# One transfer for the second group's x, and four tap products ahead of an eviction, in a fused convolution and channel-MLP kernel

## The chip, the cores and the metric

The kernel runs on one core of a Trainium2 chip. A core has five engines that run their own instruction streams: TensorE (PE, matrix products into PSUM), VectorE (DVE), ScalarE (ACT), GpSimd (POOL) and SyncE (SP, which here only issues transfers). Transfers between the chip's memory (HBM) and the core's SBUF run on 16 DMA engines; SP's transfers and POOL's transfers stand in different queues. The metric is the time of one execution on the device in microseconds (us), as a median over runs. In the profile "PEld" is TensorE's loading of weights.

## The reference

`x` is 8 x 4224 x 192 in 32-bit floats. First a causal depthwise convolution with 7 taps, whose weights are a softmax over the taps of each of 8 heads (a head is 24 neighbouring channels); then a channel MLP on the normalized result, added to it:

```
w = exp(weight - max(weight)); w = w / (sum(w) + 1e-9)          # 8 heads x 7 taps
conv[b, s, h, :] = sum over k of w[h, k] * x[b, s + k - 6, h, :]  # zero where s + k < 6
mu, var = mean and variance of conv over its 192 channels
xn  = (conv - mu) / sqrt(var + 1e-6) * g_ln
out = conv + max(xn @ w_ch1, 0) @ w_ch2                          # 192 -> 768 -> 192
```

## The kernel before

**Groups.** The sequence is cut into 18 groups of up to 16 positions on each of 128 partitions. For the whole batches a partition holds 32 neighbouring positions, which makes 4096 of the 4224; the remaining 128 positions of all eight batches together are the second group (group 1): 8 batches x 16 partitions x 8 positions. Its x is therefore not one plain run of rows: batch b goes to partitions 16b to 16b + 15, and each partition's row has its 8 positions and the 6 before them, 14 x 192 numbers or 10,752 bytes. The first group (group 0) has 6 positions, group 2 has 10, all later ones 16.

**The stages of a group.** x is loaded (`load_x`, line 133). The convolution is built up in a tile `y`: ACT writes the first tap's product for each head (`first_tap`, line 369, its instruction on line 378), and DVE adds the further taps, one instruction for each tap and head (`conv`, line 409, its instruction on line 415). DVE transposes `y` into `yt` (line 426). `up` (line 559) multiplies with the first weights in six slices f = 0 to 5 (line 531). Each slice fills four of the eight PSUM banks; ACT applies the ReLU and moves it to SBUF (`evict_up`, line 507, its instruction on line 521); slice f + 2 uses the banks of slice f. `down` (line 800, its product on line 798) multiplies with the second weights `w2`. From group 3 on other routines take this place (`up_mixed`, `down_fast`, line 861).

**The order.** The schedule is written out by hand: each engine runs its instructions in the order in which the code issues them, and waits on semaphores for what it needs. SP and POOL issue their transfers in order too; a transfer whose conditions are not met holds up those behind it.

**The start.** The weights arrive as 64-bit floats and are rebuilt as 32-bit ones on DVE and ACT (`split_words`, `scale_power`, `join_low`, `join_sign`, `join_product`, lines 231 to 268). For `w2` this happens beside the first group's `up`: its words are loaded at line 990, on SP just ahead of x for group 1 (line 994), into `raw2`. `scale_power` for `w2` is one ACT instruction (line 246), which `join_sign` on DVE needs, and which in turn comes before the product that writes `w2` (line 264).

**What ACT does beside `up(0)`.** Between the evictions of the first group's six slices ACT also evicts four copies of `w1` (`copies_of_w1`, line 348, whose products stand between slices f1 and f2 on PE and use the banks of f0 and then free them for f3), runs `scale_power` for `w2`, and makes the first tap's products of group 1, for two heads behind f0, for two behind f1, for four behind f3.

**What DVE does beside it.** `join_low`, then the taps 1 to 4 of group 1 for heads 0 and 1, then the same for heads 2 and 3 (the loop on line 1031), `join_sign` and `join_product` for `w2`, taps 5 and 6 of heads 0 to 3, the transposition of the first half of group 1's `y`, all taps of heads 4 to 7, and the second half's transposition.

**x for group 1.** `load_x(1, gate=True)` first writes one element of each partition on DVE (line 139), which the transfers then wait for, so that they start only behind DVE's earlier work. Then it issues eight transfers of 16 partitions each (line 142), those of batches 0 to 3 on SP and those of batches 4 to 7 on POOL. SP's next transfers are the store of group 0's `y` (line 487) and x for group 2 (line 151).

Of the kernel before, what the change touches and what calls it, by code (L numbers as in the profile page):

```python
# [16 lines left out]
def kernel(  # L17
# [29 lines left out]
    nc = tc.nc  # L47
    PSUM = bass.MemoryType.PSUM
    B, S, D = x.shape
    H, K = weight.shape  # L50
    F = moe_w_ch1.shape[1]
    P = 128
# [3 lines left out]
    PAD = K - 1  # L56
    J = 16
    R = 2 * J
    LEFT = (S - P * R) * B // P
    LP = P // B  # L60
# [64 lines left out]
    def take_set():  # L125
        i = (turn[0] + 3) // 4 * 4 % 8
        turn[0] = i + 4
        return all_banks[:, i : i + 4]
# [4 lines left out]
    def load_x(g, queue=nc.sync, pad=True, gate=False):  # L133
        b, j0, n = groups[g]
        t = xpool.tile([P, J + PAD, D], F32, tag="xg", name=f"xg{g}")
        xg[g] = t
        flat = t.rearrange("p j d -> p (j d)")
        if gate:
            nc.vector.memset(t[0 : 1 if b is not None else P, 0:1, 0:1], 0.0)
        if b is None:  # L140
            for b in range(B):
                (queue if b < B // 2 else nc.gpsimd).dma_start(
                    out=flat[LP * b : LP * b + LP, 0 : (PAD + n) * D],
                    in_=bass.AP(
                        tensor=x.tensor, offset=(b * S + P * R - PAD) * D,
                        ap=[[n * D, LP], [1, (PAD + n) * D]],
                    ),
                )
            return
        if j0:  # L150
            queue.dma_start(
                out=flat[:, 0 : (n + PAD) * D], in_=xr[b, :, (j0 - PAD) * D : (j0 + n) * D]
            )
            return
        if b:

            queue.dma_start(
                out=flat[:, 0 : (PAD + n) * D],
                in_=bass.AP(
                    tensor=x.tensor, offset=(b * S - PAD) * D, ap=[[R * D, P], [1, (PAD + n) * D]]  # L160
                ),
            )
            if pad:
                nc.gpsimd.memset(t[0:1, 0:PAD, :], 0.0)
            return
        nc.gpsimd.memset(t[0:1, 0:PAD, :], 0.0)
        for p0, p1 in ((16, P), (1, 16)):
            nc.sync.dma_start(  # L168
                out=flat[p0:p1, 0 : (PAD + n) * D],
                in_=bass.AP(  # L170
                    tensor=x.tensor, offset=(b * S + p0 * R - PAD) * D,
                    ap=[[R * D, p1 - p0], [1, (PAD + n) * D]],
                ),
            )
        nc.sync.dma_start(out=flat[0:1, PAD * D : (PAD + n) * D], in_=xr[b, 0:1, 0 : n * D])
# [38 lines left out]
    for s in range(2):  # L214
        nc.sync.dma_start(  # L215
            out=raw1[:, s].rearrange("p f w -> p (f w)"),
            in_=w1_words[0:P, 2 * FH * s : 2 * FH * (s + 1)],
        )
    for r in range(2):
        nc.sync.dma_start(  # L220
            out=raw1[Q * r : Q * r + Q, 2, :, :].rearrange("p f w -> p (f w)"),
            in_=w1_words[P:D, 2 * FH * r : 2 * FH * (r + 1)],
        )
    load_x(0)


# [18 lines left out]
    def scale_power(power):  # L245
        nc.scalar.activation(power, power, AF.Relu, scale=float(1 << 23), bias=low)
# [52 lines left out]
    for q in range(NQ):  # L299
        m = copy[C * q : C * q + C].rearrange("p (q i) -> p q i", q=NQ)  # L300
        nc.gpsimd.affine_select(
            out=m, in_=m, pattern=[[0, NQ], [-1, C]],
# [9 lines left out]
        out=unit, in_=unit, pattern=[[-1, P]], compare_op=ALU.not_equal, fill=1.0, base=0,  # L312
# [56 lines left out]
    def first_tap(g, heads=(0, H)):  # L369
        n = groups[g][2]  # L370
        if g == 1:

            y[g] = y[0][:, groups[0][2] :]
        elif heads[0] == 0:
            y[g] = ypool.tile([P, J, D], F32, tag="y", name=f"y{g}")
        for h in range(*heads):
            cs = slice(h * GRP, h * GRP + GRP)
            nc.scalar.mul(y[g][:, 0:n, cs], xg[g][:, 0:n, cs], taps[:, h, 0:1])  # L378
# [30 lines left out]
    def conv(g, k0=1, k1=K, heads=(0, H)):  # L409
        n = groups[g][2]  # L410
        t = xg[g]
        for k in range(k0, k1):
            for h in range(*heads):
                cs = slice(h * GRP, h * GRP + GRP)
                nc.vector.scalar_tensor_tensor(  # L415
                    out=y[g][:, 0:n, cs], in0=t[:, k : k + n, cs], scalar=taps[:, h, k : k + 1],
                    in1=y[g][:, 0:n, cs], op0=ALU.mult, op1=ALU.add,
                )
# [72 lines left out]
    def hidden_tile(g):  # L491
        n = groups[g][2]

        if fast[g]:
            ht[g] = room.rearrange(
                "p (h e f q j t) -> p h e f q j t", h=2, e=2, f=FC, q=NQ, t=width(g)
            )
        else:
            ht[g] = room[:, 0 : NF * NQ * n * C].rearrange(
                "p (f j q t) -> p f j q t", f=NF, q=NQ, t=C  # L500
            )
# [57 lines left out]
    def up(g):  # L559


        n = groups[g][2]
        hidden_tile(g)
        for f in range(NF):
            banks = take_set()
            rows_of_tiles(banks, yt[g][:, 0:n], w1[:, :, f * P : f * P + P])
            evict_up(g, f, banks[:, :, 0 : n * C])
            if g == 0 and f == 0:
                first_tap(1, heads=(0, H // 4))
            elif g == 0 and f == 1:  # L570
                copies_of_w1(1, [(q, 1) for q in range(NQ)])
                first_tap(1, heads=(H // 4, H // 2))
            elif g == 0 and f == 2:
                scale_power(words_2[2])
            elif g == 0 and f == 3:
                first_tap(1, heads=(H // 2, H))
            between(g, f)

    def quarters_of_w1(f0=0, f1=FC):
# [5 lines left out]
    def let_in(tile):  # L585

        nc.vector.memset(tile[0:1, 0:1, 0:1], 0.0)
# [395 lines left out]
    for s in range(3):  # L983
# [7 lines left out]
        out=raw2.rearrange("p (c d) w -> p c (d w)", d=D),  # L991
        in_=w2_words.rearrange("(c p) d -> p c d", p=P),
# [25 lines left out]
    for g in range(NG):  # L1018
        mixed, last = g in MIXED, g + 1 == NG
        if g + 2 < NG and g not in (1, 2, 3):  # L1020
            load_x(g + 2)
        if mixed:
            work = up_mixed(g, ahead(g), pending)
            pending = iter(())
        else:
            up(g)
            work = []
        if g == 0:
            early = CH * C // GRP
            join_low(*words_2)  # L1030
            for h in range(0, early, 2):
                conv(1, 1, 5, heads=(h, h + 2))
            join_sign(*words_2)
            join_product(w2flat, *words_2)
            conv(1, 5, K, heads=(0, early))
            transpose(1, 0, CH)
            conv(1, heads=(early, H))
            first_tap(2)
            second_tap(2)
            let_in(w1sums[:, 1])  # L1040
            transpose(1, CH, NC)
            moments(0)
            moments(1)
            load_x(3, gate=True)
            store_y(1)
            sums_of_quarters(w1sums[:, 1], w12, w22)
            sums_of_quarters(w1sums[:, 0], w11, w1sums[:, 1])
            next(root(0, True))
        elif g == 1:
            conv(2, 2)  # L1050
            transpose(2)
            first_tap(3)
            add_second_tap(3, 6)
            sums_of_quarters(w2sums[:, 2], b12, b22)
            sums_of_quarters(w2sums[:, 0], b12, b11)
            sums_of_quarters(w2sums[:, 1], b22, w2sums[:, 0])
            sums_of_quarters(w2sums[:, 3], b21, w2sums[:, 1])
            load_x(4, nc.gpsimd, pad=False)
            store_y(2, nc.gpsimd)
        elif g == 2:  # L1060
            conv(3, 2, 5, heads=(0, 6))
            lower_sum(2)
            conv(3, 5, K, heads=(0, 6))
            let_in(w1sums[:, 2])
            sums_of_quarters(w1sums[:, 2], w21, w1sums[:, 0])
        if g < 2:
            down(g)
            if g == 1:
                moments(2)
                next(root(2, True))  # L1070
                conv(3, heads=(6, H))
            continue
        if g > 2 and g + 2 < NG:
            store_y(g + 1)
        results = down_fast(g, work)
        if last:
            finish_fast(g, 1, *results)
            for j in range(fast[g]):
                add(g, j, ots[g][:, j])
            store(g, 0, fast[g])  # L1080
            for j in range(fast[g], groups[g][2]):
                rows = take_bank()[:, 0:D]
                down_row(rows, lambda f: rows_left[g][:, f, j - fast[g]])
                add(g, j, rows)
                store(g, j, j + 1)
        else:
            if g % 2 or g + 2 == NG:
                pending = root(g + 1 - g % 2)
# [30 lines left out]
```

## Time and profile before

The median of three runs is 949.84 us (949.24 to 950.11). The profile is of one execution of 948.92 us, whose span from the first to the last instruction is 947.1 us; 1.8 us lie around it. The TensorE clock was granted in full.

| what (from the profile's span start) | us |
|---|---|
| span | 947.1 |
| first product of the first group's `up`, f0 and f1 | 22.20 to 26.38 |
| products for the copies of w1 | 26.81 to 28.38 |
| f2 to f5 | 28.40 to 36.48 |
| first group's `down` | 36.41 to 48.38 |
| second group's `up` begins | 48.31 |
| DVE: `join_low` for w2 | 25.03 to 26.39 |
| DVE: taps 1 to 4 of group 1, heads 0 and 1, then heads 2 and 3 | 27.34 to 30.08, 30.30 to 33.03 |
| DVE: w2 written | 35.70 |
| DVE: transposition of group 1's second half | 47.25 to 48.23 |
| ACT: power scaling for w2 | 31.41 to 32.66 |

How to read it: the page gives busy time for each engine; the chain of waits follows the work that ended last back to the start; the list of waits names who waited for whom and how long; the timeline lists instructions in order with start, duration, and the idle time just before with what ended it, in square brackets. "issue" there means that the profile shows no releaser. One 32-bit product of PE appears as two records. Transfers are listed with the engine that issued them and the time from issue to landing.

### The profile page before, as it was taken

Reading aid. Unit: us, or ns where it says so; the run is one execution under the profiler, and the core shown is the slowest. Engines: PE = TensorE matmul, PEld = TensorE weight load, DVE = VectorE, ACT = ScalarE, POOL = GpSimd, SP = SyncE. Lnnn points to the kernel's source line nnn. Section 1 sums busy time; section 2 is a strip of 40 time slices with the busy share of each in tenths; the row PEclk is TensorE's granted clock in tenths of the full one; section 3 lists DMA queues with packets and bytes.
Section 4 is the critical chain, followed back from the end, with each engine's and each line's share of the span. In section 5 each row is a group of like instructions: output and inputs, shape, how many; then the busy total and the mean of one; then the engine's idle time right before and its main releaser. Section 6 shows DMA issues by size and latency. Waiting matters only on the chain.

```text
span 947.1 us, 38072 instructions
## 1 busy us (share of the span) xinstructions
PE 939.3 (99%) x16900; PEld 751.3 (79%) x16900; DVE 894.2 (94%) x1498; ACT 699.8 (74%) x1250; POOL 342.1 (36%) x478
## 2 busy tenths in 40 slices
PE   8999999999999999999999999999999999999998
PEld 6998896877869687786989778696867869596787
DVE  8999999999999999999999999999999999999867
ACT  7753688596878969687896968779696877867362
POOL 2158422713145141533227141452316231261420
PEclk9999999999999999999999999999999999999999
DMA  8359589689797988979697897979889797778261
GB/s 210 109 151 218 104 235 275 123 191 229 135 271 133 251 164 187 220 132 279 132 248 152 201 219 129 278 133 252 161 198 208 131 275 137 174 137 133 54 114 68
DMA packets 39833, 169.35 MB, mean 179 GB/s; under 512 B 4469, under 2 KB 8182, under 8 KB 33655
## 3 DMA queue, kind: packets, MB, share of 16 engines
q0 software_dynamic: 32992, 107.46, 61.2%
q1 hardware_dynamic: 6672, 59.47, 16.9%
q8 instruction: 132, 2.16, 0.9%
q14 instruction: 31, 0.25, 0.1%
q10 hardware_dynamic: 6, 0.00, 0.0%
HBM read 38.93 MB, written 50.33 MB: 94 GB/s over the span
## 4 chain that ended last, share of the span: by engine, by line
PE 98%; DMA 1%; SPq 0%; issue 0%; DVE 0%
PE ps L531 49%; PE ps L861 44%; PE ps L798 4%; DMA xg<-in_x_dram 1%; PE ps L326 1%; PE ps L352 0%; PE ps L355 0%; PE ps L338 0%; SPq L220 0%; SPq L215 0%; SPq L168 0%; DVE y L955 0%
## 5 line engine op out<-in xcount | busy, mean ns | idle before, releaser
L415 DVE SCALAR_TENSOR_TENSOR y<-xg,taps,y 128x384 f32<-128x384 f32 (+3 forms) x720 | 364.7, 583 | 3.2 <-DMA y<-room 1.3
L861 PE MATMUL ps<-room,w2sums 128*32 128x256 f32 (+2 forms) x4608 | 245.2, 371 | 0.0
L531 PE MATMUL ps<-yt,w 32*128 32x256 f32 (+2 forms) x4160 | 237.7, 373 | 0.0
L531 PEld LDWEIGHTS ps<-yt,w 32*128 32x128 f32 x4160 | 210.7, 185 | 21.5 <-issue 6.7
L861 PEld LDWEIGHTS ps<-room,w2sums 128*32 128x32 f32 x4608 | 154.6, 110 | 84.7 <-issue 0.4
L662 ACT COPY room<-ps 128x512 f32<-128x512 f32 (+1 forms) x213 | 174.2, 859 | 62.3 <-PE ps L531 62.1
L861 PE MATMUL ps<-room,w 128*32 128x256 f32 (+2 forms) x3456 | 188.8, 371 | 0.0
L828 DVE TENSOR_TENSOR room<-room 128x1024 f32<-128x1024 f32 (+2 forms) x147 | 161.2, 1172 | 21.4 <-PE ps L861 12.0
L861 PEld LDWEIGHTS ps<-room,w 128*32 128x32 f32 x3456 | 113.7, 110 | 67.0 <-DVE room L668 5.0
L531 PE MATMUL ps<-ysums,w1sums 32*128 32x256 f32 x2160 | 126.7, 376 | 0.0
L531 PEld LDWEIGHTS ps<-ysums,w1sums 32*128 32x128 f32 x2160 | 116.3, 185 | 4.9 <-issue 0.2
L951 POOL DMA_DIRECT2D out_dram<-ot x69 | 58.9, 938 | 162.3 <-ACT ot L940 158.5
L867 ACT COPY cs<-ps 128x256 f32<-128x256 f32 (+2 forms) x192 | 70.3, 368 | 45.0 <-PE ps L861 44.8
L407 POOL DMA_DIRECT2D y<-tb x59 | 52.1, 1373 | 138.3 <-ACT room L867 104.7
L675 ACT ACTIVATE room<-room 128x1024 f32<-128x1024 f32 (+1 forms) x89 | 94.3, 1073 | 3.3 <-DMA room<-parts_cs 3.2
L940 ACT ACTIVATE ot<-ot,r 128x192 f32<-128x192 f32 x224 | 94.7, 468 | 0.0
L378 ACT ACTIVATE y<-xg,taps 128x384 f32<-128x384 f32 (+3 forms) x141 | 73.0, 606 | 1.6 <-issue 1.2
L446 DVE BATCH_NORM_STATS2 st<-y 128x6 f32<-128x192 f32 x264 | 70.1, 343 | 0.0
L531 PE MATMUL ps<-yt,w1sums 32*128 32x256 f32 x1080 | 69.1, 376 | 0.0
L867 ACT COPY room<-ps 128x256 f32<-128x256 f32 (+2 forms) x96 | 35.5, 371 | 44.5 <-PE ps L861 43.7
L531 PE MATMUL ps<-ysums,w 32*128 32x256 f32 x1080 | 68.3, 374 | 0.0
L396 ACT ACTIVATE tb<-xg,taps 128x384 f32<-128x384 f32 (+1 forms) x120 | 66.1, 630 | 0.0
(120 smaller groups left out, 933.8 us busy)
## 6 DMA issues: line engine op xcount, KB each, us to landing
xg<-in_x_dram SPq DMA_DIRECT2D x14, 2112.0 KB, 15.9
room<-room POOLq DMA_DIRECT2D x45, 512.0 KB, 5.2
out_dram<-ot POOLq DMA_DIRECT2D x59, 384.0 KB, 9.5
y<-tb POOLq DMA_DIRECT2D x58, 384.0 KB, 8.7
out_dram<-y SPq DMA_DIRECT2D x13, 1536.0 KB, 9.5
room<-parts_cs POOLq DMA_DIRECT2D x28, 512.0 KB, 6.9
room<-parts_tb POOLq DMA_DIRECT2D x14, 1024.0 KB, 7.6
xg<-in_x_dram POOLq DMA_DIRECT2D x1, 2112.0 KB, 13.7
```

Source lines behind the costliest of these rows:

```text
L378: nc.scalar.mul(y[g][:, 0:n, cs], xg[g][:, 0:n, cs], taps[:, h, 0:1])
L396: nc.scalar.mul(tb[g][:, 0:n, cs], xg[g][:, 1 : 1 + n, cs], taps[:, h, 1:2])
L415: nc.vector.scalar_tensor_tensor(out=y[g][:, 0:n, cs], in0=t[:, k : k + n, cs], scalar=taps[:, h, k : k + 1], in1=y[g][:, 0:n, cs], op0=AL ...
L446: nc.vector.bn_stats(out=sums[g][:, j, :], in_=y[g][:, j, :])
L531: nc.tensor.matmul(banks[:, q, i * w + j1 * t : i * w + j2 * t], right[rows, c, P * i : P * i + P], left[rows, j1:j2, c, :], start=start, ...
L662: nc.scalar.activation(to, of, AF.Relu) if relu else nc.scalar.copy(to, of)
L675: nc.scalar.activation(c, c, AF.Relu)
L828: nc.vector.tensor_tensor(a[:, *dst, f], a[:, *left, f], a[:, *right, f], op=op)
L861: nc.tensor.matmul(dst[C * q : C * q + C, 0:w], right[:, f, C * c : C * c + C], left[:, f, q], start=(first and f == PAIR), stop=(f == PAI ...
L867: nc.scalar.copy(to[:, c], dst[:, 0:w].rearrange("p (j t) -> p j t", t=t))
L940: nc.scalar.mul(ots[g][:, j, :], ots[g][:, j, :], rstd[g][:, j : j + 1])
L951: nc.gpsimd.dma_start(out=rows[:, d0:d1], in_=src[:, d0:d1], accum_op=ALU.add)
```

## The change

It has three parts. (1) `load_x` for group 1 issues one transfer of 128 partitions on SP instead of four on SP and four on POOL; its source is given as 8 batches x 16 rows x 2688 numbers. (2) The first tap's products of group 1 are placed differently between the evictions of the first group: four heads behind f0, none behind f1, two each behind f2 and f3; the power scaling for `w2` moves from behind f2's eviction to behind the copies of w1. (3) Taps 1 to 4 of heads 0 to 3 of group 1 are one run (tap by tap over four heads) instead of two runs of two heads.

```diff
@@ load_x
         if b is None:
-            for b in range(B):
-                (queue if b < B // 2 else nc.gpsimd).dma_start(
-                    out=flat[LP * b : LP * b + LP, 0 : (PAD + n) * D],
-                    in_=bass.AP(
-                        tensor=x.tensor, offset=(b * S + P * R - PAD) * D,
-                        ap=[[n * D, LP], [1, (PAD + n) * D]],
-                    ),
-                )
+            queue.dma_start(
+                out=flat[:, 0 : (PAD + n) * D],
+                in_=bass.AP(
+                    tensor=x.tensor, offset=(P * R - PAD) * D,
+                    ap=[[S * D, B], [n * D, LP], [1, (PAD + n) * D]],
+                ),
+            )
             return
@@ up
             if g == 0 and f == 0:
-                first_tap(1, heads=(0, H // 4))
+                first_tap(1, heads=(0, H // 2))
             elif g == 0 and f == 1:
                 copies_of_w1(1, [(q, 1) for q in range(NQ)])
-                first_tap(1, heads=(H // 4, H // 2))
-            elif g == 0 and f == 2:
                 scale_power(words_2[2])
-            elif g == 0 and f == 3:
-                first_tap(1, heads=(H // 2, H))
+            elif g == 0 and f < 4:
+                first_tap(1, heads=(2 * f, 2 * f + 2))
             between(g, f)
@@ behind the first group's up
             early = CH * C // GRP
             join_low(*words_2)
-            for h in range(0, early, 2):
-                conv(1, 1, 5, heads=(h, h + 2))
+            conv(1, 1, 5, heads=(0, early))
             join_sign(*words_2)
             join_product(w2flat, *words_2)
             conv(1, 5, K, heads=(0, early))
```

## The prediction

> **What bounds the kernel now.** I read the page first: how busy the engines are, and the chain that ended last.
>
> ```profile
> span 947.1 us, 38072 instructions
> PE 939.3 (99%) x16900; PEld 751.3 (79%) x16900; DVE 894.2 (94%) x1498; ACT 699.8 (74%) x1250; POOL 342.1 (36%) x478
> ...
> PE 98%; DMA 1%; SPq 0%; issue 0%; DVE 0%
> ```
>
> PE is the bound and almost never rests. Next I asked who made PE wait; this is the whole list:
>
> ```profile
> PE ps L211 <- DMA room<-in_weight_dram: 2.1, 1, 2.1
> PE ps L335 <- DVE raw L989: 0.6, 1, 0.6
> PE ps L326 <- DMA xg<-in_x_dram: 0.5, 1, 0.5
> PE ps L352 <- issue: 0.4, 1, 0.4
> ```
>
> The first three waits end by 12.4 us, before the changed transfer is issued (12.6 us). The last is a gap before 26.81 us. After 28.40 us the chain of waits is PE alone up to 942.99 us. So whatever shifts the start of the third slice of the first group (below: f2) at 28.40 us shifts the end by as much, and nothing else in this change can, as long as the other engines keep up. The timeline from 24 to 29 us shows what sets that start:
>
> ```profile
> 24.86 0.83 ACT L521 ACTIVATE room<-ps 128x768 f32<-128x768 f32 x1
> ...
> 26.81 0.93 PE L352 MATMUL ps<-room 32*128 32x384 f32 x8 [0.42 <-issue]
> ...
> 26.85 0.80 ACT L378 ACTIVATE y<-xg,taps 128x192 f32<-128x192 f32 x2 [1.16 <-issue]
> ...
> 27.56 0.79 ACT L521 ACTIVATE room<-ps 128x768 f32<-128x768 f32 x1
> ...
> 28.40 0.78 PEld L531 LDWEIGHTS ps<-yt,w 32*128 32x128 f32 x17 [0.64 <-ACT room L521]
> ```
>
> ACT evicts slice f0 (24.86), idles 1.16 us, multiplies two heads of x1 (the second group's x; 26.85), evicts f1 (27.56), and only then are f2's banks free: f2's weight load waited 0.64 us on that eviction. PE's own work (copies of w1, 26.81 to 28.38) ends at the same moment, so two paths tie. The idle 1.16 us is the wait for x1, which the view of line 142 confirms:
>
> ```profile
> L142 SPq DMA_DIRECT2D xg<-in_x_dram x4: 332/410/417, 12.6 to 13.9; - x4
> L142 POOL DMA_DIRECT2D xg<-in_x_dram x4: 504/517/693, 12.9 to 14.6; - x4
> ...
> DMA to landing us min/median/max: 7.6/9.4/12.0
> ```
>
> The last piece is issued by POOL at 14.6 and takes 12.0: it lands at 26.6, and ACT goes on 0.22 us later. Why so slow? Two stretches compared, one with x1's pieces alone, one with the next load of x (x2, one transfer of 128 rows) and the store of y:
>
> ```profile
> 17.00:23.00 6.00, 6.00 (x70) 4.20 (x72) 6.00 (x19) 3.59 (x11) 0.00 (x0) 1.00 1.00 170
> 25.00:30.00 5.00, 4.56 (x92) 3.73 (x88) 4.02 (x9) 3.85 (x9) 0.00 (x0) 1.00 0.83 344
> ```
>
> The last two columns are the busy share of the DMA engines and GB/s. x1's 16-row pieces keep all 16 engines busy yet move 170 GB/s, or 10,752 B x 16 / 170 = 1.01 us a row; the later stretch moves 344 / 0.83 = 414 GB/s of busy time, or 0.41 us for such a row. The queues of the first stretch:
>
> ```profile
> q0 software_dynamic: 94, 0.55, 53.7%
> q1 hardware_dynamic: 101, 0.47, 46.2%
> ```
>
> SP's queue (q1) had half of the engines' time.
>
> **The change, part by part.** *The four taps.* From the rows above f1's eviction follows the landing L of x1 so: ACT starts at L + 0.22, each head takes 0.355 (26.85 to 27.56 for two), and f2 starts 0.84 after the eviction begins. Before: 26.63 + 0.22 + 2 x 0.355 + 0.84 = 28.40. With four heads: f2 = L + 2.48. PE's own path gives 28.40, or 27.98 if its gap of 0.42 closes. So the taps are free when L is at most 25.9, and each us of L above that is a us of the end. The power scaling (1.25 us on ACT, moved from behind f2's eviction to before it) and the heads 4 to 8 (two and two instead of four behind f3) fall into ACT's waits for PE: a slice is 2.02 us of PE (8.08 / 4) against at most 0.8 + 1.25 of ACT, and f2's banks are wanted only by f4. Cost nothing; without that cover at most 1.25 + 0.7.
>
> *One run of 16 on DVE.* The same 16 products (2.74 + 2.73 us in the two runs before). Merged they lose the wait of 0.22 between the runs. The 24 products of four heads took 7.95, or 0.331 each against 0.342: another 0.2. DVE must have w2 ready (35.70 now) when PE begins down at 36.4; it starts from L too, so a late x1 delays both, DVE by 0.22 + 0.49 + 16 x 0.342 + 2.7 after L (about L + 8.9), PE by L + 2.48 + 8.08 = L + 10.6. PE stays last. The second transpose, 12.5 us behind w2, comes at L + 21.4 and PE wants it at L + 22.5. Nothing added.
>
> *One transfer instead of eight.* Removed: four issues on POOL (2.16 us; POOL's next work is at 43.8, so nothing) and three on SP (some 1.2 us; SP's next issue, y0's store, waits for DVE until 21.4: nothing). Seven semaphore waits fewer on ACT and DVE: at most the 0.2 between 26.65 and 26.85, and only if x1 is still what ends the wait. The bytes are the same 1.376 MB; all of them now go through SP's queue, behind w2's load, whose packets leave the engines near 16.0. What decides is the pace. The bounds, from this trace: at best that of x2's stretch, 1.376 MB / 414 GB/s = 3.3 us, landing by 16.0 + 3.3 + 0.5 = 19.8; at worst SP's queue goes on as it did in the stretch 17 to 23, 0.47 MB in 6 us = 78 GB/s, 17.6 us, and with the 2 us from the last data to the landing that x1's pieces show, L = 35.6.
>
> Which end is nearer? The later loads of x have 128 rows in one plain walk on both sides. This one has 128 rows at the destination, but its source stays a walk of eight blocks of 16 rows: the built instruction carries 8 x 16 x 2688 on that side, because the blocks lie 811,008 elements apart and can't be merged. I take it to be shared out by blocks, eight lanes of 16 rows. Then rows that now go over 16 engines go over eight, and one lane moves 16 rows in succession: 16 x 0.41 = 6.6 us if a row is as fast as x2's, 16 x 1.01 = 16.2 us if it is as slow as x1's are now, 8.1 us if today's 170 GB/s is a ceiling on all lanes together. The data, the rows written and their neighbours are those of the slow pieces, so I stay on that side and take the middle of 8.1 and 16.2, 12.2 us, with 1.5 to the landing: L = 16.0 + 12.2 + 1.5 = 29.7.
>
> [...]
>
> *The sum.* f2 = 29.7 + 2.48 = 32.2 instead of 28.4: +3.8 us; the gap of 0.42 lies inside this wait. y0's store and x2 stand behind x1 in SP's queue: 2.15 MB at 414 GB/s is 5.2 us, so x2 lands near 34, and ACT wants it at 37.3 + 3.8. On the profiled execution: 948.92 (span 947.1 and 1.8 around it) + 3.8 = 952.7; on the median of the runs, 949.84, 0.92 above that execution, 953.6.
>
> **The rivals.** *Spread like x2* (0.38): the rows are dealt over the engines so that no two write next to each other, 3.3 to 6.6 us, L = 19.8 to 24.6. ACT then goes straight from f0's eviction (next start 25.60) to four taps, f1's eviction at 27.02, f2 at 27.98 behind PE's copies if the gap closes: -0.42, so 949.4; if the gap is PE's own, 28.40 and 949.8. For it: every 128-row load here is fast. Against it: the shape of the source. A landing between 25.9 and 27.8 belongs here too, at up to +1.9. *Faster than the noise* (0.05): -1.9 us or more, 947.9 or below. Against it: PE idles 0.42 us in the only place that is touched, and every later stretch is PE's own work. It needs unprofiled runs that lose much more there than the profiled one. *Slower* (0.57) is the forecast: its place is ACT's wait ahead of the first tap, its price L - 25.9, and it decides from L = 25.9 on. A worse form of it, 16.2 us or more of data, gives L = 34.2 and +8.3: 958.1.
>
> **How the numbers follow.** About 0.2% (1.9 us) is what a measurement of this kernel can tell from no change. Slower by more: L above 27.8, 0.57. Within: 0.38. Faster: 0.05. The likeliest gives 953.6, with its own range 951.6 to 957.6 (data in 10.2 to 16.2 us). The whole range has to take in the rival at 949.4: 949.0 to 957.0, which leaves out the worse form and gains beyond 0.8 us.
>
> **What would show it.** Right: in the profile after, ACT and DVE idle until about 29 to 32 us ahead of the first tap of x1, f1's eviction follows four taps later, PE has a wait of 2 to 6 us before f2 put down to ACT L521, and the stretch from 17 to 28 shows the DMA engines half busy at 85 to 130 GB/s. Wrong: the first tap follows f0's eviction at 25.6 without idle time and the stretch from 16 to 21 moves over 200 GB/s; then the time is 949.4 to 949.8. Also wrong: PE waiting in down (line 798) for w2, or before up of the second group for its transpose.

## The result, and the profile after

The changed kernel takes 957.97 us (median of four runs, 956.50 to 958.43), the kernel before 949.85 (949.24 to 950.11). The ratio is 1.0085, 95% interval 1.0073 to 1.0097: 8.1 us slower. The forecast was slower, 953.6 (+3.8) with a range of 949.0 to 957.0: the sign and the place were right, the size was less than half of what came, and the time lies above the range. The profiled execution took 957.52 us, its span is 955.5, 8.4 more than before.

Line numbers from line 142 on are one to three lower in the changed kernel. The list of what PE waited for now has a new head (columns as before: total us, times, longest):

```profile
PE ps L530 <- ACT room L520: 5.8, 1, 5.8
PE ps L210 <- DMA room<-in_weight_dram: 2.1, 1, 2.1
PE ps L858 <- DVE room L665: 0.2, 1, 0.2
```

The new head is one wait of 5.8 us, for ACT's eviction in front of f2. The timeline of the changed kernel from 24 to 36 us, ACT and PE rows, shows how it comes about (start, duration, what; in brackets the idle time before):

```profile
25.26 0.83 ACT L520 ACTIVATE room<-ps 128x768 f32<-128x768 f32 x1
...
27.06 0.83 PE L354 MATMUL ps<-room 32*128 32x384 f32 x8
31.49 1.49 ACT L377 ACTIVATE y<-xg,taps 128x192 f32<-128x192 f32 x4 [5.39 <-DMA xg<-in_x_dram]
...
32.88 0.79 ACT L520 ACTIVATE room<-ps 128x768 f32<-128x768 f32 x1
...
33.73 2.62 PE L530 MATMUL ps<-yt,w 32*128 32x192 f32 x28 [5.83 <-ACT room L520]
```

ACT is done with f0 at 26.1 and then idles 5.39 us for x1, which the profile now names: the one transfer, issued at 12.7, lands near 31.3. Four taps, f1's eviction, and f2 starts at 33.73 instead of 28.40. PE had finished the copies at 27.9; its own gap of 0.42 ahead of them is gone, but that is hidden in the wait. How x1 came in, in two stretches of the changed kernel (last three columns: granted TensorE clock, busy share of the DMA engines, GB/s):

```profile
17.00:22.00 5.00, 5.00 (x49) 3.69 (x51) 5.00 (x18) 3.06 (x10) 0.00 (x0) 1.00 0.50 116
22.00:28.00 6.00, 5.89 (x124) 4.80 (x116) 4.31 (x6) 3.38 (x6) 0.00 (x0) 1.00 1.04 214
```

From 17 to 22 us half of the DMA engines' time is used, at 116 GB/s, where before all of it was, at 170. From 22 us on the store of y0 and x2 run beside x1.

PE's clock was 1.00 at this place before (first PE's busy time, then its weight loads, DVE, ACT, POOL; then the clock):

```profile
28.40:36.40 8.00, 8.00 (x192) 7.79 (x192) 7.75 (x19) 7.04 (x14) 0.00 (x0) 1.00 0.10 39
```

In the changed kernel, in stretches from the wait on:

```profile
27.40:33.70 6.30, 0.49 (x8) 0.00 (x0) 1.72 (x6) 2.21 (x6) 0.00 (x0) 0.86 0.70 224
33.70:36.00 2.30, 2.27 (x28) 2.28 (x32) 2.30 (x9) 2.30 (x5) 0.00 (x0) 0.50 0.17 73
36.00:38.00 2.00, 2.00 (x32) 2.00 (x28) 2.00 (x6) 0.33 (x1) 0.00 (x0) 0.50 0.00 0
38.00:40.00 2.00, 2.00 (x44) 2.00 (x44) 1.97 (x3) 1.49 (x3) 0.00 (x0) 0.81 0.00 0
40.00:44.00 4.00, 4.00 (x108) 3.96 (x100) 3.97 (x12) 2.30 (x4) 0.00 (x0) 1.00 0.02 4
```

PE comes back from its wait at half speed and is at full speed again some 5 us later. Its rows of f2 to f5 take 10.53 us instead of 8.08. Where the 8.4 us of the two profiles lie:

| PE begins | before | after | later by |
|---|---|---|---|
| first group's `up` | 22.20 | 22.52 | 0.32 |
| f2 | 28.40 | 33.73 | 5.33 |
| first group's `down` | 36.41 | 44.19 | 7.78 |
| second group's `up` | 48.31 | 56.09 | 7.78 |
| end of the span | 947.1 | 955.5 | 8.4 |

So 5.33 us are the delay of f2 by the wait, 2.45 the clock, and 0.6 come behind the start of the second group's `up`. Their cause is open: the list of waits shows only 0.2 us there, and the runs of the kernel before differ by 0.9 among themselves. Nothing behind f2 takes any of the delay back.

### The profile page after: what moved, and what is told of

It reads as the page before. It is cut to its first block, busy times and chain, and to the rows that moved or that the text cites. A ratio compares the mean times of both kernels' runs of the same rounds, so it can differ in the third digit from the quotient of the medians.

```text
span 955.5 us, 38056 instructions
## 1 busy us (share of the span) xinstructions
PE 943.5 (99%) x16900; PEld 750.8 (79%) x16900; DVE 894.0 (94%) x1498; ACT 699.8 (73%) x1250; POOL 340.2 (36%) x474
## 4 chain that ended last, share of the span: by engine, by line
PE 66%; DVE 0%; issue 0%
PE ps L858 34%; PE ps L530 32%; PE ps L795 1%; DVE y L952 0%
## 5 line engine op out<-in xcount | busy, mean ns | idle before, releaser
L530 PE MATMUL ps<-yt,w 32*128 32x256 f32 (+2 forms) x4160 | 240.4, 376 | 5.8 <-ACT room L520 5.8
L530 PEld LDWEIGHTS ps<-yt,w 32*128 32x128 f32 x4160 | 213.6, 187 | 26.9 <-issue 6.5
L858 PEld LDWEIGHTS ps<-room,w2sums 128*32 128x32 f32 x4608 | 151.6, 110 | 87.6
```

Source lines behind the costliest of these rows:

```text
L530: nc.tensor.matmul(banks[:, q, i * w + j1 * t : i * w + j2 * t], right[rows, c, P * i : P * i + P], left[rows, j1:j2, c, :], start=start, ...
L858: nc.tensor.matmul(dst[C * q : C * q + C, 0:w], right[:, f, C * c : C * c + C], left[:, f, q], start=(first and f == PAIR), stop=(f == PAI ...
```

## The experiments

All times are beside runs of the kernel before on the same chip in the same batch (medians 949.71, 949.64, and one run of 950.78).

**Which part costs: e1 and e2.** e1 is the kernel before with part 1 alone, e2 with parts 2 and 3 alone.

```diff
 e1, against before
-            for b in range(B):
-                (queue if b < B // 2 else nc.gpsimd).dma_start(
...
+            queue.dma_start(
+                out=flat[:, 0 : (PAD + n) * D],
...
 e2, against the changed kernel: the same lines the other way round
```

> Before with part 1 alone (one transfer), taps as before. Theory: the transfer runs on eight lanes of 16 rows and lands near 31.4 us, as in the changed kernel; f2 starts 0.22 + 2 x 0.355 + 0.84 = 1.77 us later, at 33.2, 4.8 us later than before, and PE's clock falls to half after the long wait: +4.8 + 2.4 = about +7.2 us, 957.0. Rival (the four taps ahead of the eviction, or the longer run on DVE, carry most of it): within 2 us of before, 949 to 952.

> Before with parts 2 and 3 alone (four taps, one run), eight transfers as before. Theory: x1 lands at 26.6 as before, two more heads stand ahead of f1's eviction, f2 starts at 26.63 + 2.48 = 29.1, +0.7 us: 950.5. [...] Rival (the taps carry the loss): +4 us or more, 954 and up, with the clock at half.

e1: 956.73 us, ratio 1.0079 (1.0064 to 1.0094), as expected. ACT idled 4.45 us for x1, the first tap began at 30.95, f2 at 32.50, and f2 to f5 took 9.76 us:

```profile
32.50 9.76 PE L530 MATMUL ps<-yt,w 32*128 32x192 f32 x192 [4.20 <-ACT room L520]
```

e2: 949.57, ratio 1.0004 (0.9993 to 1.0014): the expected +0.7 us is inside that interval, so the times can't tell it. In its first profile (952.54 us) the whole start stood 3.8 us later ahead of the changed place, where PE's clock was 0.50 from 12.5 to 19.2 us; a second profile of the same kernel:

> The same kernel as e2 (parts 2 and 3 alone), for a second profile, since in the first the whole start stood 3.8 us later ahead of the changed place. Theory: ACT waits for x1 until 26.6, four taps, f2 at 29.1 (0.7 later than before), no loss of clock.

949.34 us. Its list of PE's waits has this row:

```profile
PE ps L531 <- ACT room L521: 0.7, 1, 0.7
```

The four taps do hold up f1's eviction by 0.7 us as worked out, but f2 came at 28.66, not 29.1: x1 was used from 26.43 on, and PE's gap of 0.42 was absent. Against before that is +0.3. The transfer alone costs 7.0 of the 8.1 us, and the taps alone are within the noise. Whether the remaining 1.1 us belong to the two together the times can't tell, since the intervals of e1 and of the changed kernel overlap; in the profiles the changed kernel's f2 is 1.23 us later than e1's, 0.54 by x1's first use and 0.7 by the two more heads ahead of the eviction.

**Why the transfer is slow: e3, e8.** e3 keeps one transfer, four taps and one run, and lays the second group's rows out so that the batch runs fastest over the partitions (its stores then take every eighth partition). e8 takes a plain walk; it reads the rows behind batch 0 instead of the reference's, so only its time and trace are of use.

```diff
 e3, against the changed kernel
-                    ap=[[S * D, B], [n * D, LP], [1, (PAD + n) * D]],
+                    ap=[[n * D, LP], [S * D, B], [1, (PAD + n) * D]],
...
-            (slice(LP * b, LP * b + LP), left[b, :, j1 * D : j2 * D]) for b in range(B)
+            (slice(b, P, B), left[b, :, j1 * D : j2 * D]) for b in range(B)
 e8, against the changed kernel
-                    ap=[[S * D, B], [n * D, LP], [1, (PAD + n) * D]],
+                    ap=[[n * D, P], [1, (PAD + n) * D]],
```

> The changed kernel with the second group's rows laid out with the batch running fastest over the partitions (row l of batch b on partition 8 l + b), so that the source of the one transfer is 16 x 8 x 2688 instead of 8 x 16 x 2688; the stores of this group take every eighth partition. Theory (the outer dimension of the source sets the number of engines): 16 engines, 8 rows each, x1 lands between 20 and 24 us, ACT goes from f0's eviction straight to the four taps, no loss of clock: 949.4 (949.0 to 949.9). Rival (one transfer from eight separate regions of HBM, or one queue, is slow in itself): lands near 31 again, 957 to 958.

> The changed kernel with the source of the one transfer as a plain walk of 128 rows, 1536 numbers apart, instead of 8 x 16 rows: same bytes, same row length, same partitions, but the rows are those behind batch 0, so that group 1 is computed from other rows of x than the reference's. Theory (the block form of the source alone makes the pace): rows at 0.41 us on 16 engines, 3.3 us for all, DMA at about 400 GB/s from 16 us, landing near 20, no wait of PE, 949.4. Rival (overlapping rows of 10,752 bytes, or queueing behind w2's load, make it slow): landing beyond 26.

e3: 949.58 us, ratio 0.9997 (0.9988 to 1.0006). e8: 949.72, one run. The same stretch of e3 as above, and the first one of e8:

```profile
17.00:22.00 5.00, 5.00 (x50) 3.40 (x48) 5.00 (x17) 2.93 (x9) 0.00 (x0) 1.00 0.93 202
```

```profile
16.00:18.00 2.00, 2.00 (x20) 1.72 (x18) 2.00 (x8) 2.00 (x7) 0.00 (x0) 1.00 1.01 426
```

Same bytes, one queue, one transfer: with 16 as the source's outer dimension 15 of the 16 engines' worth of time is used instead of 8 (the packets of the traces have 15.6 rows under way at a time from 18 to 22 us, and 8.1 in the changed kernel), and with a plain walk the engines also move twice as much each. In e3 ACT goes from f0's eviction straight into the taps and f2 comes 0.55 us before that of the kernel before:

```profile
25.58 1.51 ACT L377 ACTIVATE y<-xg,taps 128x192 f32<-128x192 f32 x4
26.96 0.83 ACT L520 ACTIVATE room<-ps 128x768 f32<-128x768 f32 x1
```

So the rival (one queue, or eight separate regions of HBM, slow in themselves) falls.

**Is it the number of engines, and what sets a row's time: e9, e10, e7.** e9 issues two transfers of four batches each, e10 four of two, all on SP.

```diff
 e9 (step 4) and e10 (step 2), against the changed kernel
-            queue.dma_start(
-                out=flat[:, 0 : (PAD + n) * D],
+            for b in range(0, B, 4):
+                queue.dma_start(
+                    out=flat[LP * b : LP * (b + 4), 0 : (PAD + n) * D],
...
-                    ap=[[S * D, B], [n * D, LP], [1, (PAD + n) * D]],
+                        ap=[[S * D, 4], [n * D, LP], [1, (PAD + n) * D]],
```

> The changed kernel with two transfers on SP, of four batches (64 partitions) each, in place of the one. [...] Rival (engines are not set by the block count): lands at 31 or before, 958 or less.

> The changed kernel with four transfers on SP, of two neighbouring batches (32 partitions) each. [...] Rival (a row takes 0.8 us for a reason of the engine or of HBM): 26 GB/s, 52 us, landing near 69, about 995.

965.74 and 972.15 us (one run each). The stretch from 18 to 22 us of e9, and of e10:

```profile
18.00:22.00 4.00, 4.00 (x42) 2.84 (x42) 4.00 (x15) 2.34 (x7) 0.00 (x0) 1.00 0.26 69
```

```profile
18.00:22.00 4.00, 4.00 (x42) 2.90 (x38) 4.00 (x13) 1.91 (x5) 0.00 (x0) 1.00 0.13 54
```

A quarter and an eighth of the engines' time: four engines, then two, and 4.0 and 2.0 rows under way at a time, though the same bytes stand in the same queue. In these runs the number followed the outer dimension of the source: 2, 4, 8 and 16 gave 2.0, 4.0, 8.1 and 15.6 rows under way. With two engines a row takes 2 x 10,752 B / 54 GB/s = 0.40 us, as in e8 with sixteen (16 x 10,752 / 426 = 0.40). By the packets from 18 to 22 us a row took 0.65 us on average with e9's four engines, 0.74 with the eight of the changed kernel and 0.79 with e3's sixteen. Twice the engines from e10 to e9 brought 69 GB/s instead of 54, since a row took 0.65 us instead of 0.40. e9's first tap began at 39.65 us and e10's at 45.18. The packets show where they parted: e9's rows took between 0.4 and 0.8 us up to 27 us, up to 1.3 beside y0's store and x2, and mostly 0.41 from 33 us on; e10's took 0.41 except between 25 and 30 us, beside y0's store and x2, where they took 0.8.

e7 asks whether the place of the rows that are written together matters: it deals the eight pieces of the kernel before to the two queues so that they write 32 partitions apart instead of 64.

```diff
 e7, against before
-                (queue if b < B // 2 else nc.gpsimd).dma_start(
+                (queue if b % 4 < 2 else nc.gpsimd).dma_start(
```

> Before, with the eight transfers dealt differently over the two queues: batches 0, 1, 4, 5 on SP and 2, 3, 6, 7 on POOL, so that the two queues write partitions 32 apart at the same time instead of 64 apart. Same bytes, same number of transfers and engines. [...] Rival (the pace comes from the HBM side or from each engine): 170 GB/s again, lands at 26.6, 949.8.

949.27 us, ratio 0.9997 (0.9987 to 1.0006). From 16 to 24 us it moved 167, 172, 129 and 141 GB/s in stretches of 2 us, before 191, 167, 177 and 171; the first tap began at 27.58 instead of 26.85. Slower than before: by the packets a row took 1.12 us from 18 to 22 us, before 0.99. The two queues were not in step (by 18 us SP's had begun 30 rows and POOL's 12), so most of the blocks that met were not those that had been paired. So e7 does not show whether the place matters; that a row can take longer with more engines at work rests on e9 and e10 (0.65 against 0.40 us), and why it does is not shown.

**What stands behind x1: e5.** y0's store and x2's load are issued behind DVE's sixteen products.

```diff
 e5, against the changed kernel
-    store_y(0)
...
-        if g + 2 < NG and g not in (1, 2, 3):
+        if g + 2 < NG and g not in (0, 1, 2, 3):
...
             conv(1, 1, 5, heads=(0, early))
+            load_x(2, gate=True)
+            store_y(0)
```

> The changed kernel with the store of y0 and the load of x2 issued only behind DVE's sixteen products, so that x1 has the DMA engines for itself. Theory (x1's rows take 0.81 us in pairs and were held up to 1.3 us from 22 us on by the store and x2, which eight idle engines had started): x1's rows stay at 0.81, 16 x 0.81 = 12.9 us from 16.0, landing near 30 instead of 31.5, f2 1.5 us earlier; PE waits some 4.3 us, so part of the clock's loss may go too: 1.5 to 3.5 us less than the changed kernel, 954.5 to 956.5. Rival (what stands behind x1 does not touch it): lands at 31.4 again, 957 to 958.4.

955.01 us, ratio 1.0052 (1.0036 to 1.0068): 5.4 us over its runs of before, where the changed kernel has 8.1. The second stretch:

```profile
22.00:28.00 6.00, 6.00 (x124) 4.76 (x116) 4.51 (x6) 3.38 (x6) 0.00 (x0) 1.00 0.51 121
```

```profile
29.75 1.49 ACT L377 ACTIVATE y<-xg,taps 128x192 f32<-128x192 f32 x4 [3.67 <-DMA xg<-in_x_dram]
```

Without the other two transfers eight engines go on at 121 GB/s; the first tap begins at 29.75 instead of 31.49 (though x1 was issued 0.6 us later here) and f2 at 31.98. PE's wait is 3.94 us, and f2 to f5 take 9.68.

**The clock: e4 and e4b.** Twenty products of 128 x 128 fill PE's wait.

```diff
 e4b, against the changed kernel (e4: the same behind the copies, into columns that they leave free)
             elif g == 0 and f == 1:
+                for _ in range(20):
+                    nc.tensor.matmul(all_banks[:, 1, 0:P], less, less, start=True, stop=True)
                 copies_of_w1(1, [(q, 1) for q in range(NQ)])
```

> The changed kernel with 20 products of 128 x 128 into unused columns of a PSUM bank, between the copies of w1 and f2, so that PE works through about 5 of the 5.8 us of its wait; their results are not used. Theory (the idle time lowers PE's clock to half for the first 5 us of work after it, 2.4 us lost): the clock stays at 1.00, f2 to f5 take 8.1 instead of 10.5 us: 2.4 us less than the changed kernel, 955.5. Rival (f2 to f5 are slow because ACT or DVE are late, or the clock falls at this time anyway): no gain, 957.5 to 958.4.

> The changed kernel with 20 products of 128 x 128 into a free bank ahead of the copies of w1 (not behind them, where in the run before they had to wait for ACT), 5 us of PE work inside its wait; their results are not used. Theory (5.8 us without work lower PE's clock to half for the first 5 us after it, 2.4 us): the clock stays at 1.00, f2 to f5 take 8.1 us, 2.4 us less than the changed kernel: 955.5. Rival (f2 to f5 are slow for another reason): 957.5 to 958.4.

e4: 964.22 us, ratio 1.0156 (1.0139 to 1.0173), a miss: the products did not run inside the wait but behind it, since they wait for ACT to evict the copies that lie in the same bank:

```profile
PE ps L572 <- ACT w L359: 6.6, 1, 6.6
```

e4b: 955.24 us, ratio 1.0063 (1.0046 to 1.0080): 5.6 us over its runs of before instead of 8.1. Its PE timeline:

```profile
26.36 4.73 PE L571 MATMUL ps<-room 128*128 128x128 f32 x40
31.02 0.93 PE L351 MATMUL ps<-room 32*128 32x384 f32 x8
31.77 0.82 PE L354 MATMUL ps<-room 32*128 32x384 f32 x8
32.99 8.08 PE L530 MATMUL ps<-yt,w 32*128 32x192 f32 x192 [0.40 <-ACT room L520]
```

x1 still comes late (ACT idles 5.01 us, and the first tap begins at 30.75, 0.74 earlier than in the changed kernel, which is part of the gain), but PE has work, its clock stays at 1.00, and f2 to f5 take their 8.08 us. The late x1 and the clock are two separate costs.

## Why the prediction was right in kind and wrong in size

**The bound and the place.** Right. The chain is PE alone behind f2, and the delay at f2 is found again at every later stage and at the end.

**The relation f2 = L + 2.48.** Right: the taps begin at 31.49, which puts L near 31.3 (with the prediction's 0.22 taken over), and f2 is at 33.73. Between them, four heads took 1.39 us (1.42 worked out) and the rest 0.85 (0.84).

**The moves that were costed at nothing.** Right. The power scaling, the regrouped heads 4 to 8 and the fewer issues on POOL and SP made nobody wait: in the changed kernel's list PE's only other wait at the start is the one for the weights (2.1 us, as before), DVE wrote w2 at 40.0, ahead of `down` at 44.19, and the second transpose ended at 52.6, ahead of 56.09.

**One transfer on eight lanes.** Right, and the deciding step, though "shared out by blocks" was the author's estimate from the form of the built instruction, which no run had shown: the DMA engines were half busy from 17 to 22 us, at 116 GB/s, between the 85 and 130 named. The prediction named the stretch up to 28; from 22 on the share was 1.04. The later runs bear it out: outer dimensions of the source of 16, 8, 4 and 2 gave 0.93, 0.50, 0.26 and 0.13 of the engines' time. What makes x1's rows slow is not shown. They took 0.40 us on e10's two engines, 0.65 on e9's four, 0.74 on the eight of the changed kernel and 0.79 on e3's sixteen, but 0.40 on sixteen in e8's plain walk.

**The landing.** Mis-sized: 29.7 worked out (16.0 + 12.2 + 1.5), 31.3 measured; by the packets x1's rows ran from 15.7 to 30.3 us, 14.6 instead of 12.2. The step that failed is "y0's store and x2 stand behind x1 in SP's queue". They do so only on the eight engines that x1 uses; the other eight took their shares from 22 us on (the DMA engines' share is 0.50 until then and 1.04 behind it), and x1's rows, 0.8 us before, took 0.91 from 24 to 26 us and 1.24 from 26 to 28 (medians). e5 shows it: with those two out of the way x1's rows take 12.8 us in all, and the first tap begins at 29.75, against 30.75 to 31.49 in the four runs of the one transfer that have them (e1, e4, e4b and the changed kernel). That 12.2, the middle between 8.1 and 16.2, came near these 12.8 is partly luck.

**The sum.** The step that failed for the size is "+3.8 us" itself: it passed a wait of PE on as a delay of the same length. PE stood still for 5.8 us and came back with the clock at 0.50, and 10.53 - 8.08 = 2.45 us are lost in the rows behind the wait. That term was missing altogether; e4b, where PE has work while x1 is late, loses none of it. With the landing (5.33 instead of 3.8) and the clock (2.45) the sum is 7.8, and the 0.6 that stay open make the 8.4. With the landing alone put right the forecast would have been 955.1, still inside its range, so the clock is the larger miss. Each wait of 3.94 us and more ahead of f2 came with a loss of clock in these runs (the last section has the table), and the prediction had not weighed it. Length alone does not explain every fall: in e2's first profile the clock fell at 12.5 us, and no wait of PE in the 6 us before was longer than 1.15.

**The forecast of the worse form** (16.2 us of data, 958.1) met the time by chance: the data took 14.6 us, and the rest was the clock. The measured time is also above the 957.6 up to which the prediction let its likeliest case go.

**The rivals.** "Spread like x2" is what e3 and e8 do, and they give the 949.4 to 949.8 foreseen for it (949.58 and 949.72). That the gain of a fast x1 would be too small to measure holds as well: e3 starts f2 0.55 us sooner and its interval of 0.9988 to 1.0006 contains no change. No version beat both kernels measurably.

## What to carry to other kernels

Before merging transfers, look at the outer dimension of the source as the built instruction has it, not at the number of partitions, which was 128 in the changed kernel and in e3 alike: eight blocks of sixteen rows used 0.50 of the DMA engines' time, sixteen of eight 0.93, and choosing which index runs fastest over the partitions cost nothing (e3: 949.58 us, ratio 0.9997). A transfer on the way to a wait of the bound engine is then priced in two terms, the delay and what the engine's clock loses: here 5.33 and 2.45 us, with a wait of 5.8. And a product meant to hold PE's clock at 1.00 through a wait must write to a bank that nobody has to empty first: e4's products waited 6.6 us for ACT, while e4b's, in a free bank, ran ahead of f2 and the clock stayed at 1.00.

## What the runs showed of the hardware that was not expected

The loss of clock did not grow with the wait in these runs. The traces record when the granted clock changed:

| run | PE's wait before f2, us | clock at 0.50, us in all | of these behind the start of f2 | f2 to f5, us |
|---|---|---|---|---|
| e4b | 0.40 | 0 | 0 | 8.08 |
| e5 | 3.94 | 3.41 | 3.3 | 9.68 |
| e1 | 4.20 | 3.41 | 3.4 | 9.76 |
| changed kernel | 5.83 | 6.83 | 5.0 | 10.53 |
| e9 | 13.77 | 13.65 | 3.8 | 9.90 |
| e10 | 19.65 | 20.48 | 4.7 | 10.37 |

In the five that lost clock it was at half for one, two, four or six times 3.41 us, and what f2 to f5 lose (1.60 to 2.45 us) is half of the time at 0.50 that lies behind the start of f2. So here the price followed from when such a period ended and not from how long PE had waited. How long PE may wait without loss is not settled: 1.89 us ahead of the copies (e7) cost nothing, with the clock at 1.00 from 26 to 37 us, in e4 the clock fell 2.7 us after PE's last product, and in e2's first profile it fell though no single wait was longer than 1.15 us.

Transfers of one queue ran beside each other: in the changed kernel the DMA engines' share rose from 0.50 to 1.04 at 22 us, when y0's store and x2, issued behind x1 on the same queue, started while x1 was still 9 us from landing.
